# Pooled attention and a top-1 expert layer on one core: where the experts' tiles start in SBUF, when the second slot's weights are split, and where the last slots' tests stand

## The chip, the cores and the metric

The kernel runs on one core of a Trainium2 chip. The core has five engines that run side by side: TensorE (PE in the profile; its weight loads are PEld), VectorE (DVE), ScalarE (ACT), GpSimd (POOL) and SyncE (SP, which here only starts transfers). The on-chip memory SBUF has 128 partitions; PE writes its results to PSUM, in banks of 512 float32 per partition. The metric is the device time of one execution in microseconds (us), the median of several runs.

## The reference

Two layers follow each other. Attention over 8 batches, 8 heads, 576 rows of 64 numbers: keys and values are averaged over groups of 8 rows, and each query attends to the 72 averages. Its output, 4608 tokens of 512 numbers, goes through a layer of 8 experts, of which each token takes one:

```python
logits = x @ w_gate + modality_bias[modality_id]
e_idx = np.argmax(logits, axis=1)
...
gate_w = probs[np.arange(N), e_idx]
for e in range(E):
    mask = e_idx == e
    ...
    h = np.maximum(x[mask] @ w1[e], 0.0)
    out[mask] = gate_w[mask, None] * (h @ w2[e])
```

w1 of an expert is 512 x 1024, w2 is 1024 x 512. With the inputs given, only three experts get tokens: expert 6 gets 2289, expert 7 gets 1186, expert 1 gets 1133. The first token belongs to expert 6.

## The kernel before

**Attention and routing** fill the first part of the program (lines 190 to 1028). Attention writes its rows to a buffer in device memory (xs), and routing numbers each token's place among the tokens of its expert.

**Slots.** The experts' part works in slots of 256 tokens of one expert. Slots of one expert follow each other; the first expert is that of token 0, the others come in rotation. The first two slots (EARLY_SLOTS) are filled from the tokens routed first, so that they can start before all of attention is done. Up to 27 slots are provided for; how many are used is known only at run time. With these inputs the last used one (number 17) takes 256 tokens and up to 128 more, and is called the wide slot below (function wide).

**Precision by parts.** A float32 product is built from three products of rounded parts. A tile is split into a high part (rounded copy) and a low part (the difference to the original): for weights hl[f][:, 0] and hl[f][:, 1], for tokens the two parts of xhl, for activations hh and hlo.

**One slot** runs over eight blocks f of 128 hidden units. For each f:
- first_wide: four matmuls (line 186, high weights times both parts of the tokens, 512 columns) and four (line 189, low weights times the high part, 256 columns) into a PSUM bank hp. Then ACT copies one half (L191), DVE adds the other (L192), ACT applies the ReLU and rounds (L193, tile hh), DVE writes the rest (L195, tile hlo).
- second, one f behind: for each of two 128-token tiles, three matmuls (line 1239) with hh, hh and hlo as the stationary tile and the high, low and high part of w2's block as the moving one, 512 columns, accumulated over f into a bank op.
So PE runs hidden(f), second(f-1), hidden(f+1), and so on; the chain L191, L192, L193, L195 for f has the time of second(f-1) and hidden(f+1) to finish. The wide slot uses line 176 in the place of 186 and 189, with 384 columns; its activations for f from 3 on are kept in tiles hx, those before in hh and hlo.

**Around it.** A slot's tokens are gathered by POOL (L142), scaled by POOL (L153), transposed by PE (L166) and split by ACT (L168) and DVE (L169) into xhl while the slot before runs, at f=5 or 6. Even slots use xhl0, odd ones xhl1. A slot's outputs are scaled (L1210 on DVE, L1212 on ACT) and scattered to the output by POOL (L1216).

**Weights.** The raw weights of the next slot's expert are loaded by SP into raw, and split in place for the next slot as soon as a block has been used: renew(f) puts split_hi (L136, ACT) right away, and split_lo (L139, DVE) together with the next load into a list, lag, one entry of which is taken at each following step. From slot 2 on, the split stands under a condition: flags[s+1], loaded by slot_flag into registers of ACT and DVE (L1193), says whether slot s+1 has another expert than slot s. In slot 1 the splits are always done:

```python
        def changed(fn):
            if s < EARLY_SLOTS:
                fn()
                return
            with tc.If(flags[s + 1] > 0, preferred_fallthrough_block=False):
                fn()
```

**Small work with a fixed place.** Routing's last steps and the tables of token numbers are a list of operations by place, late[(slot, f)], issued by do_late right after hidden(f). At (2, 1) stands a DVE comparison over 1584 elements (L1100), and at (3, 5) 22 small DVE operations, halves + last_half, which say how the last slots are to be run. Their results are read at the end of the program only.

**Order.** [...]

**Places in SBUF.** A pool lays its tiles out one behind the other, each rounded up to 32 bytes. Per partition, the tiles that matter start at these bytes: xhl0 26272 (160 modulo 512); xhl1 149056 (64); hh0, hh1, hlo0, hlo1 from 165504 in steps of 1536 (128); hx from 184032 in steps of 1536 (224); hl, the split weights, from 83520 in steps of 8192 (64). xhl1, hh and hlo are wide enough for the wide slot, so an ordinary slot leaves a gap in each of their rows. The experts' tiles lie over those of attention, which are done with by then.

Of the kernel before, what the change touches and what calls it, by code (L numbers as in the profile page):

```python
# [31 lines left out]
def kernel(  # L32
# [16 lines left out]
    E, _, FF = w1.shape  # L49
# [17 lines left out]
    cp = ctx.enter_context(tc.tile_pool(name="cp", bufs=1))  # L67
# [19 lines left out]
        raw[f] = cp.tile([P, 2 * D], F32, tag=f"raw{f}", name=f"raw{f}")  # L87

    xg = [cp.tile([P, XW], F32, name=f"xg{i}") for i in range(4)]
    xhl = [cp.tile([P, ND, 2, SLOT], F32R, name="xhl0")]  # L90
    arow = cp.tile([P, NT, P], BF16, name="arow")
    oh = cp.tile([P, NT, E], BF16, name="oh")
    cum = cp.tile([P, len(GROUPS) + 1, E], BF16, name="cum")
    gate = cp.tile([P, NT], F32, name="gate")
    rh = cp.tile([P, NT], F32, name="rh")
    idw = cp.tile([P, 2, NT], BF16, name="idw")
    gidx = cp.tile([P, NCOL], I32, name="gidx")
# [5 lines left out]
    adjv = cp.tile([P, E], F32, name="adjv")  # L103
    e0oh = cp.tile([P, E], F32, name="e0oh")
    lmat = cp.tile([P, E, E], F32, name="lmat")
    tri = cp.tile([P, P], BF16, name="tri")
    ones = cp.tile([P, P], BF16, name="ones")
    sel0 = cp.tile([P, P], BF16, name="sel0")
    sc1 = cp.tile([P, NT, E], F32, name="sc1")
# [46 lines left out]
    def scale(s, xgs):  # L156
        for tt in range(2):
            scale_tile(xgs[(2 * s + tt) % 4])

    def x_transposes(s, xgs, tts=(0, 1)):  # L160
        ab = xhl[s % len(xhl)]
        for tt in tts:
            x = xgs[(2 * s + tt) % 4] if tt < 2 else xgs[4]
            pt = ps_tr.tile([P, ND, P], F32, tag="tr", name=f"xt_{s}_{tt}")
            for d in range(ND):
                nc.tensor.transpose(pt[:, d, :], x[:, d * P:(d + 1) * P], ident)  # L166
            sl = slice(tt * P, (tt + 1) * P)
            nc.scalar.copy(ab[:, :, 0, sl], pt)  # L168
            nc.vector.tensor_sub(ab[:, :, 1, sl], pt, ab[:, :, 0, sl].bitcast(F32))  # L169
# [41 lines left out]
    with ExitStack() as actx:  # L211
# [737 lines left out]
        for n in range(N + 1):  # L949
            has, nxt, nxt2 = n < N, n + 1 < N, n + 2 < N  # L950
# [80 lines left out]


    mp = ctx.enter_context(tc.tile_pool(name="mp", bufs=1))
    xhl.append(mp.tile([P, ND, 2, SLOT + P], F32R, name="xhl1"))
    xg.append(mp.tile([P, XW], F32, name="xe"))
    xe = xg[4]
    ps_hp = ctx.enter_context(tc.tile_pool(name="ps_hp", bufs=1, space=PSUM))
    ps_op = ctx.enter_context(tc.tile_pool(name="ps_op", bufs=1, space=PSUM))
    op = [[ps_op.tile([P, 512], F32, name=f"op{i}_{z}") for z in range(2)] for i in range(2)]
    hp = [ps_hp.tile([P, 512], F32, name=f"hp{i}") for i in range(2)]  # L1040
    hts = [mp.tile([P, SLOT], F32, name=f"ht{i}") for i in range(2)]
    hhs = [mp.tile([P, SLOT + P], F32R, name=f"hh{i}") for i in range(2)]
    hlos = [mp.tile([P, SLOT + P], F32R, name=f"hlo{i}") for i in range(2)]


    cf = mp.tile([P, E], F32, name="cf")
# [106 lines left out]
    for i, r in enumerate(EXTRA):  # L1153
# [19 lines left out]
        (0, 5): lr[21:] + columns,  # L1173
        (1, 0): first_cols[:3] + changes,
        (1, 2): first_cols[3:],
        (3, 5): halves + last_half,
    }
    t = table(c4 + 6, NCOL, 4)
    for i, at_ in enumerate(((2, 1), (2, 3), (2, 5), (2, 7), (3, 0), (3, 1), (3, 2))):
        late[at_] = t[i:i + 1]  # L1180
# [15 lines left out]

    def part(s):

        ab = xhl[s % 2]
        o = op[s % 2]  # L1200
        third = op[(s + 1) % 2][0]
        nxt, nxt2 = s + 1 < NSLOT, s + 2 < NSLOT
        early = s + 1 < EARLY_SLOTS
# [37 lines left out]

        def changed(fn):

            if s < EARLY_SLOTS:
                fn()
                return
            with tc.If(flags[s + 1] > 0, preferred_fallthrough_block=False):  # L1247
                fn()

# [12 lines left out]

        def first_next():
            if nxt:
                first_wide(0, xhl[(s + 1) % 2], hp[0], hts[0], hhs[0][:, 0:SLOT], hlos[0][:, 0:SLOT])

        def slot0(tail):
            for f in range(NF):
# [11 lines left out]
        def run(fs, tail):  # L1280
            later = []
            for f in fs:
                def pop():
                    if len(lag) > 1 or (f == 1 and lag):
                        lag.pop(0)()
                if f:
                    hidden(f, between=pop)
                if f == 0:

                    if 0 < s < NSTAT - 1:  # L1290
                        tail(later=later)
                    else:
                        tail()
                    if nxt and EARLY_SLOTS <= s < NSTAT - 1:
                        gather(s + 1, gidx, 2 * (s + 1), xg)
                        if s == NSTAT - 2:
                            gather_tile(xe, gidx, 2 * NSTAT)
                if f == 0:
                    pop()
                do_late(s, f)  # L1300
                if f == 0 and nxt and not early and s >= EARLY_SLOTS:
                    slot_flag(s + 1)
                if f == 0 and nxt2:
                    slot_regs(s + 2)
                if s == 1 and f == 2:
                    gather(s + 1, gidx, 2 * (s + 1), xg)

                if s >= NSTAT - 1 and f == CUT and nxt:
                    gather(s + 1, gidx, 2 * (s + 1), xg)
                if f:  # L1310
                    second(f - 1)
                    renew(f - 1)
                if f == (3 if EARLY_SLOTS <= s < NSTAT - 1 else 4) and nxt and not early:
                    scale(s + 1, xg)
                    if s == NSTAT - 2:
                        scale_tile(xe)
                    while later:
                        later.pop(0)()
                if s == NSTAT - 2 and f == 4:
                    nc.gpsimd.drain()  # L1320
                if f == (5 if EARLY_SLOTS <= s < NSTAT - 1 else 6) and nxt:
                    x_transposes(s + 1, xg)
                if s == NSTAT - 2 and f == 6:
                    x_transposes(s + 1, xg, (2,))
                if f == NF - 1 and s != NSTAT - 2:
                    close()
# [37 lines left out]
        def wide(extra, close_last, tail):  # L1364

            W = SLOT + extra
            nc.vector.tensor_copy(sl, sidx[:, 2 * (s + 1):2 * (s + 1) + 1])
            at = {f: hx[f - CUT] if f >= CUT else None for f in range(NF)}
            close_last(lambda: hidden(0, at[0], W))
            tail()  # L1370
            lag.pop(0)()
            for f in range(1, NF):
                hidden(f, at[f], W)
                if lag:
                    lag.pop(0)()
                second(f - 1, (0,) if f > CUT else (0, 1, 2), at[f - 1], W)
            second(NF - 1, (0,), at[NF - 1], W)
            evac((0,))
            for tt in (1, 2):
                for f in range(CUT, NF):  # L1380
                    second(f, (tt,), at[f], W)
                if tt == 1:
                    evac((1,))
            gt = xe[0:extra, D:D + 1]
            nc.vector.tensor_scalar_mul(obl[0:extra], third[0:extra], gt)  # L1385

        return slot0 if s == 0 else run, end, evac, end_half, close, wide

    CUT = 3
    hx = [[mp.tile([P, SLOT + P], F32R, name=f"hx{i}_{z}") for z in range(2)] for i in range(NF - CUT)]  # L1390

    obl = mp.tile([P, D], F32, name="obl")
    nc.gpsimd.memset(obl, 0.0)
# [85 lines left out]
```

## Time and profile before

| | us |
|---|---|
| median of 3 runs (lowest, highest) | 619.83 (618.6, 620.39) |
| profiled execution, its own time | 619.8 |
| its span, first to last instruction | 618.1 |
| PE busy | 594.4 (96%) |
| PE weight loads busy | 511.7 (83%) |
| DVE busy | 350.0 (57%) |
| ACT busy | 280.5 (45%) |
| POOL busy | 227.9 (37%) |

In the profile's rows a matmul's length is longer than the distance to the next one, since matmuls overlap; where rates are meant, distances between starts are used. In a row of a group stand line, engine, operation, tiles written and read, shape and count, then the engine's busy time, the mean length of one in ns, and the idle time ahead of them with what ended it. In a row of the timeline stand start, length, engine and line, and in brackets the idle time before. In a row of windows stand the stretch, its length, each engine's busy time with its number of instructions, the granted PE clock, the share of the transfer engines, and GB/s. Attention takes the first 185 us or so; the slots follow from there to the end.

### The profile page before, as it was taken

The numbers are of one execution on the slowest core, as the hardware profiler recorded it, in microseconds if no ns is written. First come the engines' busy times: TensorE is split into PE (matmuls) and PEld (weight loads), VectorE is DVE, ScalarE is ACT, GpSimd is POOL, SyncE is SP. The second block draws the span as 40 slices with busy tenths as digits, with TensorE's granted clock in tenths as the row PEclk, the third lists the DMA queues.
The fourth block names the chain that finished last, engine by engine and source line by source line (L and its number), as shares of the span: only waits on it lengthen the run. The fifth ranks groups of instructions, "written<-read, shape, count | busy, mean of one in ns | idle before, by whom it ended". The sixth has DMA issues, their size and how long they took to land.

```text
span 618.1 us, 12163 instructions
## 1 busy us (share of the span) xinstructions
PE 594.4 (96%) x3663; PEld 511.7 (83%) x3663; DVE 350.0 (57%) x823; ACT 280.5 (45%) x661; POOL 227.9 (37%) x325
## 2 busy tenths in 40 slices
PE   5899999999999999999999999999999999999996
PEld 4789889888898877878888888888888888888894
DVE  6757898789958786454344345744344476434311
ACT  2667676788541553333333336433333563333210
POOL 7689969663000351403313304304304214215101
PEclk9999999999999999999999999999999999999999
DMA  9999979884202820102102155102105611102001
GB/s 248 298 307 308 361 196 367 276 266 131 65 36 79 266 69 36 54 17 71 37 34 71 50 191 172 37 32 70 37 35 159 206 48 58 35 37 86 36 2 54
DMA packets 61104, 76.33 MB, mean 123 GB/s; under 512 B 15391, under 2 KB 39967, under 8 KB 61024
## 3 DMA queue, kind: packets, MB, share of 16 engines
q1 hardware_dynamic: 55104, 55.98, 29.1%
q0 software_dynamic: 5920, 19.44, 9.6%
q8 instruction: 31, 0.51, 0.3%
q14 instruction: 49, 0.40, 0.2%
HBM read 114.94 MB, written 19.45 MB: 217 GB/s over the span
## 4 chain that ended last, share of the span: by engine, by line
PE 55%; POOLq 0%; issue 0%; DVE 0%; DVEq 0%
PE op L1239 27%; PE hp L186 16%; PE hp L189 8%; PE hp L176 3%; PE xt L166 2%; POOLq L1474 0%; DVE obl L1385 0%; DVEq L1385 0%; POOLq L1446 0%
## 5 line engine op out<-in xcount | busy, mean ns | idle before, releaser
L1239 PE MATMUL op<-hl,hh 128*128 128x512 f32 x530 | 167.1, 396 | 1.4 <-ACTq L1247 1.4
L186 PE MATMUL hp<-xhl,hl 128*128 128x512 f32 x512 | 141.0, 397 | 0.0
L192 DVE TENSOR_TENSOR ht<-ht,hp 128x256 f32<-128x256 f32 x128 | 53.9, 421 | 125.2 <-ACT ht L191 124.9
L142 POOL DMA_INDIRECT xg<-xs,gidx x36 | 39.4, 1094 | 203.2 <-ACT ht L191 138.1
L191 ACT COPY ht<-hp 128x256 f32<-128x256 f32 x128 | 47.7, 373 | 143.1 <-PE hp L189 142.8
L186 PEld LDWEIGHTS hp<-xhl,hl 128*128 128x128 f32 x512 | 94.8, 188 | 21.1
L1239 PE MATMUL op<-hl,hlo 128*128 128x512 f32 x265 | 105.2, 397 | 1.6 <-DVE hlo L195 1.5
L1239 PEld LDWEIGHTS op<-hl,hh 128*128 128x128 f32 x530 | 91.0, 188 | 13.5 <-ACTq L1247 1.6
L195 DVE SCALAR_TENSOR_TENSOR hlo<-ht,hh 128x256 fp32r<-128x256 f32 x128 | 65.9, 514 | 52.5 <-ACTq L1247 46.2
L189 PEld LDWEIGHTS hp<-xhl,hl 128*128 128x128 f32 x512 | 78.4, 188 | 11.5
L193 ACT ACTIVATE hh<-ht 128x256 fp32r<-128x256 f32 x128 | 53.5, 418 | 72.1 <-DVE ht L192 72.1
L189 PE MATMUL hp<-xhl,hl 128*128 128x256 f32 x512 | 81.5, 281 | 0.0
L1216 POOL DMA_INDIRECT out_dram<-ob,sidx x36 | 39.9, 1107 | 77.0 <-DMA out_dram<-ob,sidx 51.3
L1239 PEld LDWEIGHTS op<-hl,hlo 128*128 128x128 f32 x265 | 49.8, 188 | 15.8 <-DVE hlo L195 4.1
L638 PE MATMUL av<-vw,pt 128*128 128x146 f32 (+1 forms) x320 | 49.7, 294 | 2.3 <-DVE xb L671 1.2
L153 POOL TENSOR_TENSOR xg<-xg 128x512 f32<-128x512 f32 x32 | 36.1, 1131 | 31.6 <-DMA xg<-xs,gidx 31.4
L638 PEld LDWEIGHTS av<-vw,pt 128*128 128x128 f32 (+1 forms) x320 | 39.7, 180 | 4.8 <-ACT pt L608 2.2
L139 DVE TENSOR_TENSOR hl<-raw,hl 128x1024 fp32r<-128x1024 f32 x32 | 39.6, 1246 | 0.0
L574 PE MATMUL sc<-kt,qt 128*128 128x144 f32 x256 | 37.3, 289 | 1.0 <-ACT qt L555 1.0
L574 PEld LDWEIGHTS sc<-kt,qt 128*128 128x128 f32 x256 | 33.1, 190 | 1.7 <-ACT qt L555 0.9
L581 DVE TENSOR_REDUCE mx<-sc 128x8 f32<-128x576 f32 (+1 forms) x40 | 27.7, 691 | 8.9 <-PE sc L574 6.8
L642 PE MATMUL av<-vw,pt 128*128 128x146 f32 (+1 forms) x160 | 30.7, 291 | 0.3
(257 smaller groups left out, 821.7 us busy)
## 6 DMA issues: line engine op xcount, KB each, us to landing
raw<-in_moe_w_dram SPq DMA_DIRECT2D x288, 256.0 KB
xs<-xb SPq DMA_DIRECT2D x16, 528.0 KB
k<-in_k_dram SPq DMA_DIRECT2D x7, 1024.0 KB
v<-in_v_dram SPq DMA_DIRECT2D x7, 1024.0 KB
q<-in_q_dram SPq DMA_DIRECT2D x7, 1024.0 KB
v<-in_v_dram SPq DMA_DIRECT2D x16, 128.0 KB
xs<-xb SPq DMA_DIRECT2D x8, 132.0 KB
k<-in_k_dram SPq DMA_DIRECT2D x4, 256.0 KB
```

The source lines that it names most:

```text
L139: eng.tensor_sub(hl[f][:, 1, :], raw[f], hl[f][:, 0, :].bitcast(F32))
L142: nc.gpsimd.indirect_dma_start(out=x, out_offset=None, in_=xs[0:rows, :], in_offset=IndirectOffsetOnAxis(idx[:, col:col + 1].bitcast(U32), 0),
L186: nc.tensor.matmul(ph, hl[f][:, 0, d * P:(d + 1) * P], ab[:, d, :, 0:SLOT], start=(d == 0), stop=False)
L189: nc.tensor.matmul(ph[:, 0:SLOT], hl[f][:, 1, d * P:(d + 1) * P], ab[:, d, 0, 0:SLOT], start=False, stop=(d == ND - 1))
L191: nc.scalar.copy(t, ph[:, SLOT:2 * SLOT])
L192: nc.vector.tensor_add(t, t, ph[:, 0:SLOT])
L193: nc.scalar.activation(hh, t, AF.Relu)
L195: nc.vector.scalar_tensor_tensor(hlo, t, 0.0, hh.bitcast(F32), op0=ALU.max, op1=ALU.subtract)
L574: nc.tensor.matmul(dst, qt[:, i, :], kt[b % NB][:, :, h * SPL:(h + 1) * SPL], start=True, stop=True)
L638: nc.tensor.matmul(av[hs, u, 2 * VC * gg:2 * VC * (gg + 1)], pt[:, c, hs], vw[y][:, c].rearrange("p a x -> p (a x)"), start=(gg == 0), sto ...
L1216: nc.gpsimd.indirect_dma_start(out=out[:, :], out_offset=IndirectOffsetOnAxis(idx.bitcast(U32), 0), in_=ob, in_offset=None, bounds_check=N ...
L1239: nc.tensor.matmul(ot, l[:, ts_], hl[f][:, w, D:2 * D], start=(f == 0 and n == 0), stop=(f == NF - 1 and n == 2))
```

## The change

It has three parts.

1. **Starts of tiles.** The tiles gate (144 bytes, taking 160) and tri (256 bytes) move ahead of xhl0, which then starts at 26688, 64 modulo 512. xhl1, hh and hlo lose the extra 128 columns of the wide slot and so the gaps; the wide slot gets its own token tile xw, its activations for f before 3 go to two pairs of tiles hy, and xe, the extra rows' buffer, moves behind them. By these sizes xhl1, ht, hh, hlo, xw, hx and hy all start at 64 modulo 512. As hy has two pairs, the wide slot's order changes in one point: the three matmuls of f=2 for the third token tile move from behind hidden(3) to the end.
2. **The second slot's splits.** Slot 1's splits go under the same condition as those of later slots; the flag for slot 2 is loaded at f=1 of slot 1.
3. **The tests.** halves + last_half are issued three at a time at (3, 4), (3, 6), (3, 7) and (4, 0) to (4, 4).

```diff
     xg = [cp.tile([P, XW], F32, name=f"xg{i}") for i in range(4)]
+    gate = cp.tile([P, NT], F32, name="gate")
+    tri = cp.tile([P, P], BF16, name="tri")
     xhl = [cp.tile([P, ND, 2, SLOT], F32R, name="xhl0")]
...
-    gate = cp.tile([P, NT], F32, name="gate")
...
-    tri = cp.tile([P, P], BF16, name="tri")
...
-        ab = xhl[s % len(xhl)]
+        ab = xhl[s % len(xhl)] if s != NSTAT - 1 else xw
...
-    xhl.append(mp.tile([P, ND, 2, SLOT + P], F32R, name="xhl1"))
-    xg.append(mp.tile([P, XW], F32, name="xe"))
-    xe = xg[4]
+    xhl.append(mp.tile([P, ND, 2, SLOT], F32R, name="xhl1"))
...
-    hhs = [mp.tile([P, SLOT + P], F32R, name=f"hh{i}") for i in range(2)]
-    hlos = [mp.tile([P, SLOT + P], F32R, name=f"hlo{i}") for i in range(2)]
+    hhs = [mp.tile([P, SLOT], F32R, name=f"hh{i}") for i in range(2)]
+    hlos = [mp.tile([P, SLOT], F32R, name=f"hlo{i}") for i in range(2)]
+    CUT = 3
+    xw = mp.tile([P, ND, 2, SLOT + P], F32R, name="xw")
+    hx = [[mp.tile([P, SLOT + P], F32R, name=f"hx{i}_{z}") for z in range(2)] for i in range(NF - CUT)]
+    hy = [[mp.tile([P, SLOT + P], F32R, name=f"hy{i}_{z}") for z in range(2)] for i in range(2)]
+    xg.append(mp.tile([P, XW], F32, name="xe"))
+    xe = xg[4]
...
-        (3, 5): halves + last_half,
     }
+    tests = halves + last_half
+    for i, at_ in enumerate(((3, 4), (3, 6), (3, 7), (4, 0), (4, 1), (4, 2), (4, 3), (4, 4))):
+        late[at_] = tests[3 * i:3 * i + 3]
...
         def changed(fn):
 
-            if s < EARLY_SLOTS:
-                fn()
-                return
             with tc.If(flags[s + 1] > 0, preferred_fallthrough_block=False):
                 fn()
...
-                if f == 0 and nxt and not early and s >= EARLY_SLOTS:
+                if f == (0 if s >= EARLY_SLOTS else 1) and nxt and not early:
                     slot_flag(s + 1)
...
-            at = {f: hx[f - CUT] if f >= CUT else None for f in range(NF)}
+            at = {f: hx[f - CUT] if f >= CUT else hy[f % 2] for f in range(NF)}
...
-                second(f - 1, (0,) if f > CUT else (0, 1, 2), at[f - 1], W)
+                second(f - 1, (0,) if f > CUT else (0, 1) if f == CUT else (0, 1, 2), at[f - 1], W)
...
-                for f in range(CUT, NF):
+                for f in range(CUT + 1 - tt, NF):
                     second(f, (tt,), at[f], W)
```

More of the change, by code (lines that the diff above doesn't have):

```diff
@@ L158, in scale @@
             scale_tile(xgs[(2 * s + tt) % 4])
+    xw = None
     def x_transposes(s, xgs, tts=(0, 1)):
-        ab = xhl[s % len(xhl)]
+        ab = xhl[s % len(xhl)] if s != NSTAT - 1 else xw
         for tt in tts:
@@ L1175 @@
         (1, 2): first_cols[3:],
-        (3, 5): halves + last_half,
     }
+    tests = halves + last_half
+    for i, at_ in enumerate(((3, 4), (3, 6), (3, 7), (4, 0), (4, 1), (4, 2), (4, 3), (4, 4))):
+        late[at_] = tests[3 * i:3 * i + 3]
+    assert len(tests) <= 24
     t = table(c4 + 6, NCOL, 4)
@@ L1197, in part @@
     def part(s):
-        ab = xhl[s % 2]
+        ab = xhl[s % 2] if s != NSTAT - 1 else xw
         o = op[s % 2]
@@ L1264, in first_next @@
             if nxt:
-                first_wide(0, xhl[(s + 1) % 2], hp[0], hts[0], hhs[0][:, 0:SLOT], hlos[0][:, 0:SLOT])
+                first_wide(0, xhl[(s + 1) % 2] if s + 1 != NSTAT - 1 else xw, hp[0], hts[0], hhs[0][:, 0:SLOT], hlos[0][:, 0:SLOT])
         def slot0(tail):
@@ L1387, in part @@
         return slot0 if s == 0 else run, end, evac, end_half, close, wide
-    CUT = 3
-    hx = [[mp.tile([P, SLOT + P], F32R, name=f"hx{i}_{z}") for z in range(2)] for i in range(NF - CUT)]
     obl = mp.tile([P, D], F32, name="obl")
```

## The prediction

> **What bounds the kernel now.** I read the page first, then the tensor engine's timeline, slot by slot, because the page leaves little doubt about the engine:
>
> ```profile
> span 618.1 us, 12163 instructions
> PE 594.4 (96%) x3663; PEld 511.7 (83%) x3663; DVE 350.0 (57%) x823; ACT 280.5 (45%) x661; POOL 227.9 (37%) x325
> ...
> PE op L1239 27%; PE hp L186 16%; PE hp L189 8%; PE hp L176 3%; PE xt L166 2%; POOLq L1474 0%; DVE obl L1385 0%; DVEq L1385 0%; POOLq L1446 0%
> ...
> L186 PEld LDWEIGHTS hp<-xhl,hl 128*128 128x128 f32 x512 | 94.8, 188 | 21.1
> ...
> L1239 PEld LDWEIGHTS op<-hl,hh 128*128 128x128 f32 x530 | 91.0, 188 | 13.5 <-ACTq L1247 1.6
> ```
>
> PE is busy 96% and the chain that ended last is PE matmuls. So time can only be won by shortening PE's own steps, or by closing the few places where PE stands still. The second kind is seen against a normal step of an odd slot (here in slot 9, PE rows of the timeline; first column start, second the group's length):
>
> ```profile
> 441.36 1.09 PE L186 MATMUL hp<-xhl,hl 128*128 128x512 f32 x4
> 442.28 0.64 PE L189 MATMUL hp<-xhl,hl 128*128 128x256 f32 x4
> 442.75 0.62 PE L1239 MATMUL op<-hl,hh 128*128 128x512 f32 x2
> 443.22 0.40 PE L1239 MATMUL op<-hl,hlo 128*128 128x512 f32 x1
> 443.45 0.63 PE L1239 MATMUL op<-hl,hh 128*128 128x512 f32 x2
> ```
>
> From start to start: four L189 take 0.47, two L1239 take 0.47, one takes 0.23. A larger distance is a stall. The lengths themselves overlap and are not used.
>
> **Part 1, the tests of the last slots are spread.** In slot 3 all 22 small DVE instructions sit at f=5, ahead of the activations' transposes (L169) and the next chain L191, L192, L193, L195. First and last of the 22 on DVE, what follows there, and PE:
>
> ```profile
> 264.84 0.16 DVE L1066 TENSOR_SCALAR cg<-cf 128x8 f32<-128x8 f32 x1
> ...
> 268.51 0.14 DVE L1162 CAST meta<-lhs 1x1 int32<-1x1 f32 x1
> ...
> 270.01 0.41 DVE L192 TENSOR_TENSOR ht<-ht,hp 128x256 f32<-128x256 f32 x1
> 270.90 0.43 DVE L195 SCALAR_TENSOR_TENSOR hlo<-ht,hh 128x256 fp32r<-128x256 f32 x1 [0.48 <-ACTq L1247]
> ```
> ```profile
> 268.91 0.63 PE L189 MATMUL hp<-xhl,hl 128*128 128x256 f32 x4
> 270.92 0.73 PE L1239 MATMUL op<-hl,hh 128*128 128x512 f32 x2 [1.38 <-ACTq L1247]
> 271.49 0.39 PE L1239 MATMUL op<-hl,hlo 128*128 128x512 f32 x1
> ```
>
> The tests hold DVE for 268.65-264.84 = 3.81 us. PE goes from L189 to L1239 in 2.01 instead of 0.47, and the pair that follows takes 0.57 instead of 0.47: 1.54+0.10 = **1.64 us lost**. After the change three tests, 3 x 3.81/22 = 0.52 us, stand at each of eight steps. They hide in DVE's idle time ahead of the next L192; the tightest of these places, slot 4 f=2, has
>
> ```profile
> 282.93 0.42 DVE L192 TENSOR_TENSOR ht<-ht,hp 128x256 f32<-128x256 f32 x1 [0.70 <-ACT ht L191]
> ```
>
> 0.70 us, more than 0.52. Without that cover, PE would lose at most 0.52 us at a step. Nothing reads the tests' results before the end of the program, so nobody waits for the later ones. I take the whole 1.64; bounds 1.1 (one step uncovered) and 1.64.
>
> **Part 2, slot 1's splits under a condition.** The split of a weight tile is L136 on ACT and L139 on DVE. Its bursts:
>
> ```profile
> L136 ACT CAST hl<-raw x24: 1031/1050/1052, 203.9 to 508.9; 128x1024 fp32r<-128x1024 f32 x24
> ...
> busy tenths in 40 slices 0000000000000320000000003200000130000000
> ```
>
> Eight in slot 1, always done, and two bursts later where the expert changes. The reference with its inputs sends 2289 tokens to expert 6 (the first token's), 1186 to 7, 1133 to 1. Expert 6 fills slots 0 to 8, so slot 2 has slot 1's expert, the flag is 0, and the eight splits rewrite weights that are there already. The change drops 8 x 1.05 us on ACT and 8 L139 on DVE. Off PE that is worth only what PE waited for:
>
> ```profile
> 213.59 1.22 DVE L139 TENSOR_TENSOR hl<-raw,hl 128x1024 fp32r<-128x1024 f32 x1
> 214.72 1.27 DVE L195 SCALAR_TENSOR_TENSOR hlo<-ht,hh 128x256 fp32r<-128x256 f32 x1
> ...
> 227.66 1.80 DVE L1100 TENSOR_TENSOR bsel<-iota_f,col 128x1584 bf16<-128x1584 f32 x1
> 229.38 0.42 DVE L192 TENSOR_TENSOR ht<-ht,hp 128x256 f32<-128x256 f32 x1
> 229.71 1.74 DVE L139 TENSOR_TENSOR hl<-raw,hl 128x1024 fp32r<-128x1024 f32 x1
> 231.38 1.26 DVE L195 SCALAR_TENSOR_TENSOR hlo<-ht,hh 128x256 fp32r<-128x256 f32 x1
> ```
> ```profile
> 215.38 0.63 PE L1239 MATMUL op<-hl,hh 128*128 128x512 f32 x2
> 216.04 0.50 PE L1239 MATMUL op<-hl,hlo 128*128 128x512 f32 x1
> 216.38 0.63 PE L1239 MATMUL op<-hl,hh 128*128 128x512 f32 x2
> ```
> ```profile
> 230.59 0.63 PE L1239 MATMUL op<-hl,hh 128*128 128x512 f32 x2
> 232.69 0.50 PE L1239 MATMUL op<-hl,hlo 128*128 128x512 f32 x1 [1.46 <-DVE hlo L195]
> 233.02 0.63 PE L1239 MATMUL op<-hl,hh 128*128 128x512 f32 x2
> ```
>
> First place (slot 1): 0.66-0.47 and 0.34-0.23, that is 0.19+0.11. Second (slot 2, f=2's correction hlo): 2.10-0.47 and 0.33-0.23, 1.63+0.10. Together **2.03 us**. What is late next is read from ACT's two L191 of slot 2, f=1 and f=2:
>
> ```profile
> 225.29 0.36 ACT L191 COPY ht<-hp 128x256 f32<-128x256 f32 x1
> ...
> 228.04 0.37 ACT L191 COPY ht<-hp 128x256 f32<-128x256 f32 x1 [1.31 <-PE hp L189]
> ```
>
> From L192 to L195 it is 0.89 (rows of part 1), L195 takes 0.43. Without its three L139, DVE ends L195 of f=1 at 225.65+0.89+0.43 = 227.0, L1100 at 228.8, and runs L192 of f=2 from there, since L191 is done at 228.4; L195 starts at 229.7. PE needs it at 231.06 (230.59+0.47). Even at the 1.26 us of the quoted row it ends at 231.0, so the wait is gone or within 0.1. GpSimd, which scales tokens at that time,
>
> ```profile
> 229.33 1.04 POOL L153 TENSOR_TENSOR xg<-xg 128x512 f32<-128x512 f32 x1 [1.04 <-DMA xg<-xs,gidx]
> ```
>
> is done at 230.37; were L195 held until then, it would end at 230.8, still in time.
>
> The added wait: at f=1 of slot 1, ACT and DVE load the flag,
>
> ```profile
> L1193 ACTq TENSOR_LOAD <-meta x15: 273/276/473, 223.8 to 556.2; - x15
> ```
>
> 0.3 to 0.5 us, behind L193 and L195 of that step. Behind it stands the next L191 or L192, which waits for PE about as long; and slots 2 to 7 carry the same load and the same branches with no stall of PE. Cost 0; up to 0.2 if the load is late. Bounds of part 2: 0.3 (only the first place goes) to 2.03.
>
> **Part 3, the starts of the tiles.** In the allocation of the kernel before, every weight tile hl and the odd slots' xhl1 start at 64 modulo 512 bytes, the even slots' xhl0 at 160, hh and hlo at 128, hx at 224. After, all are at 64. The windows of slots 4 and 5, cut at the first L186 of each slot, show what goes with it:
>
> ```profile
> 272.42:295.77 23.35, 23.35 (x122) 19.68 (x120) 9.57 (x19) 7.99 (x20) 6.29 (x6) 1.00 0.14 47
> 295.77:318.99 23.22, 23.22 (x122) 19.64 (x121) 9.15 (x19) 8.11 (x20) 6.28 (x6) 1.00 0.14 48
> ```
>
> The same work at the same clock takes 23.35 in the even slot, 23.22 in the odd one: 0.13 us. If that is xhl0's start, eight even slots (2 to 16) win 8 x 0.13 = **1.0 us**. For hh, hlo and hx the nearest rows are matmuls alone with stationaries at 128 (first) and at 224 (second):
>
> ```profile
> 590.65 2.10 PE op L1239 x9
> ...
> 604.78 7.16 PE L1239 MATMUL op<-hl,hx 128*128 128x512 f32 x30
> ```
>
> 2.10/9 = 233 ns; and (7.16-0.40)/29 = 233 ns, the last one's 0.40 taken off. Two starts, one rate: I cost the stationaries' move at 0. Bounds: L186, whose stationary and (in odd slots) moving tile both start at 64, takes (442.28-441.36)/4 = 230 ns; if L1239 came to that, 3.3 ns x 840 of them in slots 1 to 17 = 2.8 us would be won, of which I allow half, 1.4, since part of the difference is where a group begins. Below, no gain in xhl0 and the odd slots as slow as the even ones: 1.0 lost. So part 3 lies between -2.4 and +1.0, and I take -1.0, the row of the very tile that moves.
>
> [...]
>
> **The rest costs nothing.** In the wide slot three L1239 move from before the first output's scatter to the end: the count on PE is the same, and the output rows in between leave 0.7 us earlier on idle engines. The new places of obl and ob lie over attention's row buffers, whose last stores must have landed before they are written. Were the first ob late, PE would meet it only when it writes the same output bank again, a slot (23 us) later.
>
> **Sum.** 1.64+2.03+1.0 = 4.7. The profiled execution has span 618.1 and its own time 619.8, so 1.7 us lie around the span. 619.8-4.7 = **615.1**. It stands 0.03 under the median of the runs, 619.83.
>
> **Rivals.**
> 1. Starts do not matter; the slot's parity does, through the output banks. For: those alternate with the slot too. Against: the nine L1239 in a row write three banks at one rate. 619.8-3.7 = 616.1. [...]
> 2. The common start helps L1239 as well: 619.8-3.67-2.4 = 613.7. For: L186's 230 ns. Against: the equal 233 at 128 and 224.
> 3. Slot 2's stall remains because L1100 alone is long enough, or another wait takes its place: 1.7 less gain, 616.8. Against: the 1.2 us of room worked out above.
> 4. The gap in xhl1's rows, not its start, made odd slots fast; closing it makes all slots slow: 619.8-3.67+1.0 = 617.1.
> 5. Slower than before: stationary and moving tile at one residue get in each other's way, the weight load outgrows its matmul and PE waits for loads at every L1239. Now 188 ns lie under 233. From a load of 233+3.67/840 = 238 ns the gain is gone; at 250 ns it costs 17 x 840 = 14 us, 630. Against: L186's loads start at 64 and take the same 188.
>
> **How the numbers follow.** Forecast 0.48, with its own range 614.4 to 615.8; rival 1 0.16, rival 2 0.16, rival 3 0.09, rival 4 0.08, rival 5 0.03. The range from 613.0 to 617.6 holds all but rival 5 and the tails. A measurement here cannot tell 0.3% (1.9 us) from no change, as the runs of before spread from 618.6 to 620.39. Faster by more, under 618.0: 0.92, all but rival 5 and a quarter of 3 and 4; within: 0.05; slower: 0.03.
>
> **What would show it.** Right: L136 16 times, none before slot 8; no PE distance over 0.5 us between L189 and L1239 in slot 3, nor between hh and hlo in slot 2; tests on DVE in threes; even slots at 23.2. Wrong: a stall at another line of slots 1 to 4; odd slots at 23.35; L1239 in a row off 233 ns; weight loads over 188 ns. A time above 617.6 or below 613.0 would mean that the tiles' starts act on PE in a way these rows do not have.

## The result and the profile after

The changed kernel takes 611.19 us (median of 4 runs, 609.76 to 611.62) beside 620.11 us (4 runs, 618.6 to 620.83) of the kernel before: a ratio of 0.9855 with a 95% interval of 0.983 to 0.9881. That is 8.9 us less where 4.7 were forecast, and the time lies under the forecast's own range (614.4 to 615.8) and under the 613.0 to 617.6 that held most of the rivals. In the profiled executions the span falls from 618.1 to 609.8 us, by 8.3.

The page after (span; busy time of PE). In the changed kernel's numbering L186, L189, L192, L195 and L1239 are L188, L191, L194, L197 and L1248, and L1100 is L1106:

```profile
span 609.8 us, 12218 instructions
...
PE 590.1 (97%) x3663; PEld 512.3 (84%) x3663; DVE 339.1 (56%) x815; ACT 273.1 (45%) x653; POOL 225.2 (37%) x325
```

PE issues as many matmuls as before, 3663, and is still the bound. So the gain is standing still that went, or matmuls that follow each other faster. Both are there.

**The three stalls are gone.** The PE rows of the timeline at the places the prediction quoted: slot 1, slot 2 and slot 3.

```profile
215.29 0.63 PE L1248 MATMUL op<-hl,hh 128*128 128x512 f32 x2
215.76 0.39 PE L1248 MATMUL op<-hl,hlo 128*128 128x512 f32 x1
...
230.02 0.63 PE L1248 MATMUL op<-hl,hh 128*128 128x512 f32 x2
230.49 0.39 PE L1248 MATMUL op<-hl,hlo 128*128 128x512 f32 x1
...
266.34 0.64 PE L191 MATMUL hp<-xhl,hl 128*128 128x256 f32 x4
266.81 0.63 PE L1248 MATMUL op<-hl,hh 128*128 128x512 f32 x2
267.28 0.39 PE L1248 MATMUL op<-hl,hlo 128*128 128x512 f32 x1
```

Each distance is 0.47 us, the normal one; they were 0.66, 2.10 and 2.01. On DVE in slot 2, where the long comparison and a low split had stood ahead of hlo:

```profile
226.41 1.80 DVE L1106 TENSOR_TENSOR bsel<-iota_f,col 128x1584 bf16<-128x1584 f32 x1
228.13 0.41 DVE L194 TENSOR_TENSOR ht<-ht,hp 128x256 f32<-128x256 f32 x1
229.03 0.53 DVE L197 SCALAR_TENSOR_TENSOR hlo<-ht,hh 128x256 fp32r<-128x256 f32 x1 [0.48 <-ACTq L1253]
```

L197 ends at 229.56, and the matmul that needs it starts at 230.49. The splits themselves (the rows of L136):

```profile
L136 ACT CAST hl<-raw x16: 1047/1050/1052, 366.0 to 502.0; 128x1024 fp32r<-128x1024 f32 x16
...
busy tenths in 40 slices 0000000000000000000000003200000130000000
```

Sixteen, none before slot 8.

**Ordinary steps are shorter, in even and odd slots alike.** The windows of slots 4 and 5, cut at the slot's first matmul as in the prediction:

```profile
268.20:291.22 23.02, 23.02 (x122) 19.65 (x121) 11.85 (x35) 8.11 (x20) 6.43 (x6) 1.00 0.15 48
291.22:314.24 23.02, 23.02 (x122) 19.65 (x121) 9.02 (x19) 8.11 (x20) 6.32 (x6) 1.00 0.15 48
```

The forecast had the even slot come down from 23.35 to the odd one's 23.22. Both are at 23.02. One step of an odd slot, PE's timeline:

```profile
291.22 1.07 PE L188 MATMUL hp<-xhl,hl 128*128 128x512 f32 x4
292.12 0.64 PE L191 MATMUL hp<-xhl,hl 128*128 128x256 f32 x4
292.60 0.63 PE L1248 MATMUL op<-hl,hh 128*128 128x512 f32 x2
...
293.98 1.07 PE L188 MATMUL hp<-xhl,hl 128*128 128x512 f32 x4
```

The odd step that the prediction quoted (it is one of slot 11, where the prediction says slot 9) ends with this row of before:

```profile
444.15 1.09 PE L186 MATMUL hp<-xhl,hl 128*128 128x512 f32 x4
```

The six L1248 take 293.98-292.60 = 1.38 us, 230 ns each, where that step had 444.15-442.75 = 1.40; the four L188 take 0.90 instead of 0.92. A step is 2.76 to 2.77 us, against 2.79 in odd slots before and 2.81 in even ones (in slot 10 the L186 start at 412.42 and 415.23).

A step is a better unit than a line in it. By the starts of single matmuls in slot 5, an odd step is shorter by 27 ns, of which 19 lie in the four L188, 1 in the four L191 and 6 in the six L1248. The pair of tiles of L188 started equal in odd slots before the change too, so what a line gains depends on its neighbours.

**Attention is untouched.** The first output matmul of slot 0 starts at 184.89 us in both profiles. DVE's last instruction on the output starts here before and here after:

```profile
612.41 0.75 DVE L1385 TENSOR_SCALAR obl<-op,xe 128x512 f32<-128x512 f32 x1 [6.68 <-PE op L1239]
```
```profile
604.18 0.75 DVE L1391 TENSOR_SCALAR obl<-op,xe 128x512 f32<-128x512 f32 x1 [6.83 <-PE op L1248]
```

So 8.23 of the 8.3 us lie in the experts' part. About 0.4 of them lie behind PE: that DVE instruction starts 0.87 us after the start of the last matmul before and 0.49 after. From the first output matmul to the start of the last one it is 7.86 us less.

### The profile page after: what moved, and what is told of

It reads as the page before. It is cut to its first block, busy times and chain, and to the rows that moved or that the text cites. A ratio compares the mean times of both kernels' runs of the same rounds, so it can differ in the third digit from the quotient of the medians.

```text
span 609.8 us, 12218 instructions
## 1 busy us (share of the span) xinstructions
PE 590.1 (97%) x3663; PEld 512.3 (84%) x3663; DVE 339.1 (56%) x815; ACT 273.1 (45%) x653; POOL 225.2 (37%) x325
## 4 chain that ended last, share of the span: by engine, by line
PE 78%; DVE 7%; POOL 5%; DMA 5%; ACT 2%; issue 2%; SPq 0%; POOLq 0%; DVEq 0%; ACTq 0%
PE op L1248 32%; PE hp L188 18%; PE hp L191 10%; DMA k<-in_k_dram 5%; PE av L640 3%; PE hp L178 3%; PE xt L168 2%; PE av L644 2%; PE sc L576 2%; PE ph L178 1%; PE pp L605 1%; POOL k L325 1%; PE pq L551 1%; DVE hl L139 1%; POOL v L325 1%
## 5 line engine op out<-in xcount | busy, mean ns | idle before, releaser
L1248 PE MATMUL op<-hl,hh 128*128 128x512 f32 x512 | 161.0, 396 | 0.0
L188 PE MATMUL hp<-xhl,hl 128*128 128x512 f32 x512 | 138.8, 393 | 0.0
L194 DVE TENSOR_TENSOR ht<-ht,hp 128x256 f32<-128x256 f32 x128 | 53.9, 421 | 124.3 <-ACT ht L193 121.2
L142 POOL DMA_INDIRECT xg<-xs,gidx x36 | 38.1, 1057 | 197.8 <-ACT ht L193 120.6
L188 PEld LDWEIGHTS hp<-xhl,hl 128*128 128x128 f32 x512 | 94.8, 188 | 19.2
L1248 PE MATMUL op<-hl,hlo 128*128 128x512 f32 x256 | 100.1, 391 | 0.2
L1248 PEld LDWEIGHTS op<-hl,hh 128*128 128x128 f32 x512 | 87.9, 190 | 11.3 <-ACT hh L195 0.3
L197 DVE SCALAR_TENSOR_TENSOR hlo<-ht,hh 128x256 fp32r<-128x256 f32 x128 | 63.3, 495 | 55.8 <-ACTq L1253 49.0
L191 PEld LDWEIGHTS hp<-xhl,hl 128*128 128x128 f32 x512 | 78.2, 189 | 10.3
L195 ACT ACTIVATE hh<-ht 128x256 fp32r<-128x256 f32 x128 | 53.6, 419 | 67.5 <-DVE ht L194 67.1
L191 PE MATMUL hp<-xhl,hl 128*128 128x256 f32 x512 | 81.2, 281 | 0.0
L1248 PEld LDWEIGHTS op<-hl,hlo 128*128 128x128 f32 x256 | 48.1, 188 | 12.6 <-DVE hlo L197 1.6
L153 POOL TENSOR_TENSOR xg<-xg 128x512 f32<-128x512 f32 x32 | 35.5, 1115 | 32.4 <-DMA xg<-xs,gidx 32.2
L139 DVE TENSOR_TENSOR hl<-raw,hl 128x1024 fp32r<-128x1024 f32 x24 | 29.0, 1219 | 0.4 <-issue 0.4
```

What stands on the lines that cost most here:

```text
L142: nc.gpsimd.indirect_dma_start(out=x, out_offset=None, in_=xs[0:rows, :], in_offset=IndirectOffsetOnAxis(idx[:, col:col + 1].bitcast(U32), 0),
L188: nc.tensor.matmul(ph, hl[f][:, 0, d * P:(d + 1) * P], ab[:, d, :, 0:SLOT], start=(d == 0), stop=False)
L191: nc.tensor.matmul(ph[:, 0:SLOT], hl[f][:, 1, d * P:(d + 1) * P], ab[:, d, 0, 0:SLOT], start=False, stop=(d == ND - 1))
L194: nc.vector.tensor_add(t, t, ph[:, 0:SLOT])
L195: nc.scalar.activation(hh, t, AF.Relu)
L197: nc.vector.scalar_tensor_tensor(hlo, t, 0.0, hh.bitcast(F32), op0=ALU.max, op1=ALU.subtract)
```

## The experiments

In other executions attention took up to 2 us more or less (the first output matmul came between 183.9 and 186.7 us). The table therefore has the experts' part alone beside the span: from that matmul to the start of the last DVE instruction on the output, both read in the timeline.

| kernel | span | experts' part | slots 4 and 5 | ratio of the times to before, same job (95%) |
|---|---|---|---|---|
| before | 618.1 | 427.52 | 23.35, 23.22 | |
| changed | 609.8 | 419.29 | 23.02, 23.02 | 0.9855 (0.983 to 0.9881) |
| tests only | 616.3 | 426.21 | 23.35, 23.21 | 0.9964 (0.9944 to 0.9983) |
| condition only | 617.5 | 425.08 | 23.31, 23.20 | 0.9963 (0.9943 to 0.9983) |
| starts only | 613.1 | 423.29 | 23.02, 23.02 | 0.9934 (0.990 to 0.9968) |
| changed, activations 64 on | 611.9 | 422.37 | 23.22, 23.21 | 0.9918 (0.989 to 0.9946) |
| changed, activations 256 on | 611.3 | 419.01 | 23.02, 23.01 | one run |
| changed, gaps back | 609.4 | 418.97 | 23.01, 23.02 | one run |
| changed, xhl0 at 160 | 609.9 | 420.11 | 23.12, 23.02 | one run |
| changed, low weights 16 on | 609.6 | 419.70 | 23.00, 23.02 | 0.9884 (0.9862 to 0.9907) |

Kernels that should be alike (changed, 256 on, gaps back) differ by 0.3 us in the experts' part, and the three kernels below that put groups behind the changed kernel's end by up to 0.7 (418.94 to 419.67). The traces show from what. Where the next expert's weights are split, two to four steps of a run take 3.1 us, because the writing of hlo (L195, L197 after) takes 1.27 us there instead of 0.42, with GpSimd's scaling of tokens (L153) at work at the same time (in before, hlo at 398.02, 494.25 and 515.02, GpSimd's rows from 397.71, 494.13 and 514.44, 2.48, 1.10 and 2.75 us long), and PE waits for it. There are three such steps in before and in changed, four with the tests only and with the low weights 16 on, two with 256 on and gaps back, and three in the other rows. So 0.3 us of a difference can be one such step more or less. The other irregular piece is the 0.4 us behind the last matmul: tests only has it as before, and all other rows have lost it, the condition alone and the starts alone among them. By what, no run shows.

### One part at a time

The theory after the first comparison: the two stall terms are right, and the tiles' starts are worth 4.6 us instead of 1.0. The rival: the three parts need each other.

```diff
-        (3, 5): halves + last_half,
     }
+    tests = halves + last_half
+    for i, at_ in enumerate(((3, 4), (3, 6), (3, 7), (4, 0), (4, 1), (4, 2), (4, 3), (4, 4))):
+        late[at_] = tests[3 * i:3 * i + 3]
```

> The kernel before with the tests spread and nothing else. Reading of the two traces: the stall of 1.54+0.10 us in slot 3 goes and nothing else changes, so 1.6 us less (span 616.5). Rival: the tests' removal from f=5 moves a wait elsewhere in slots 3 and 4, then less than 1.1 us is won.

The ratio is 0.9964, 2.2 us less (by the 95% interval 1.1 to 3.5). PE in slot 3 of this kernel (its L1242 is L1239):

```profile
268.47 0.63 PE L189 MATMUL hp<-xhl,hl 128*128 128x256 f32 x4
268.94 0.63 PE L1242 MATMUL op<-hl,hh 128*128 128x512 f32 x2
269.41 0.39 PE L1242 MATMUL op<-hl,hlo 128*128 128x512 f32 x1
```

2.01 has become 0.47 and 0.57 has become 0.47: 1.64 us, as worked out. The experts' part is shorter by 1.31, and this run has one more of the 0.3 us waits at the splits. No stall came up in slots 3 and 4.

```diff
         def changed(fn):
-            if s < EARLY_SLOTS:
-                fn()
-                return
             with tc.If(flags[s + 1] > 0, preferred_fallthrough_block=False):
...
-                if f == 0 and nxt and not early and s >= EARLY_SLOTS:
+                if f == (0 if s >= EARLY_SLOTS else 1) and nxt and not early:
```

> The kernel before with slot 1's splits under the condition and nothing else. Reading of the two traces: the stalls of 0.30 us in slot 1 and 1.73 us in slot 2 go, 2.0 us less (span 616.1). Rival: the missing splits are worth more than the stalls, because ACT and DVE also free PE's later steps; then over 2.5 us.

The ratio is 0.9963, 2.3 us (1.1 to 3.5). PE in slot 2:

```profile
231.39 0.63 PE L1239 MATMUL op<-hl,hh 128*128 128x512 f32 x2
231.86 0.39 PE L1239 MATMUL op<-hl,hlo 128*128 128x512 f32 x1
232.09 0.63 PE L1239 MATMUL op<-hl,hh 128*128 128x512 f32 x2
```

The wait of 1.63+0.10 is gone. The experts' part is 2.44 us shorter, of which 0.37 lie behind the last matmul; the other 2.07 are the stalls' 2.03. The missing splits bring nothing beyond the stalls that can be told.

For the starts alone, both edits above were taken back out of the changed kernel:

> The changed kernel with the splits of slot 1 always done and the 22 tests at one place again, so that only the tiles' starts and sizes are changed. If the three parts add up, 8.3-1.64-2.03 = 4.6 us of span are left here (span 613.5), and a step of an ordinary slot takes 2.767 us. Rival: the starts alone are worth the 1.0 us of the forecast (span 617.1, steps of 2.793) and the rest needs all three parts together.

The ratio is 0.9934, 4.1 us (2.0 to 6.2), the experts' part 4.23 us shorter, both slots at 23.02. The rival falls: the starts alone do it. One thing does not add: with a faster PE and the splits still there, the stall in slot 2 grows,

```profile
229.63 0.63 PE L1245 MATMUL op<-hl,hh 128*128 128x512 f32 x2
231.99 0.50 PE L1245 MATMUL op<-hl,hlo 128*128 128x512 f32 x1 [1.73 <-DVE hlo L197]
```

to 2.36-0.47 = 1.89 from 1.63. DVE there:

```profile
226.83 1.80 DVE L1106 TENSOR_TENSOR bsel<-iota_f,col 128x1584 bf16<-128x1584 f32 x1
...
228.88 1.87 DVE L139 TENSOR_TENSOR hl<-raw,hl 128x1024 fp32r<-128x1024 f32 x1
230.67 1.26 DVE L197 SCALAR_TENSOR_TENSOR hlo<-ht,hh 128x256 fp32r<-128x256 f32 x1
```

About half of the 0.26 us is that PE arrives earlier, 3.27 us after the start of L1106 (229.63+0.47-226.83) where it was 3.40 after that of L1100; the other half is that the chain on DVE is longer, 5.10 instead of 4.98 us, with a split of 1.87 instead of 1.74. The three experts' parts together give 1.31+2.44+4.23 = 7.98 of 8.23. To the last matmul, and with the extra wait of the tests' run and the longer stall of this one set right, they give 1.6+2.07+4.1 = 7.8 of 7.86.

### What about the starts: one matmul by itself

Behind the end of the changed kernel, groups of 32 matmuls take one weight tile as stationary and another as moving tile, each with a chosen start; their results go to no output, so that the run's whole time says nothing.

```diff
+    def probe(g, st, mv, n, count):
+        wt = hl[0].rearrange("p w c -> p (w c)")[:, st // 4:st // 4 + P]
+        mt = hl[1].rearrange("p w c -> p (w c)")[:, mv // 4:mv // 4 + n]
+        for _ in range(count):
+            nc.tensor.matmul(hp[g % 2][:, 0:n], wt, mt, start=True, stop=True)
```

> The changed kernel with 48 groups of 32 matmuls behind its end, whose results go to no output: one weight tile as stationary, another as moving tile, with the stationary's start moved in steps of 64 or 32 bytes and the moving tile's start at 64, 0, 160 or 128 modulo 512. Theory S: with the moving tile at 64, a matmul of 512 columns takes 226.7 ns with the stationary at 64 and 233.3 ns at 128 and 224. Theory R: only the difference of the two starts counts, so that 226.7 ns is found wherever both are equal, also at 0, 128 and 160. Theory A: the stationary's absolute start counts whatever the moving tile's. Theory N (gaps, not starts): all groups take the same.

Windows of this run, one group of 32 each (stretch, its length, PE's busy time). Stationary and moving start, modulo 512, are 64/64, 128/64, 192/64, 256/64, 320/64, then 0/0, 64/160 and 128/128:

```profile
602.39:609.65 7.26, 7.26 (x34) 6.01 (x33) 0.75 (x1) 0.00 (x0) 0.97 (x1) 1.00 0.11 39
609.65:617.11 7.46, 7.46 (x33) 6.01 (x32) 0.00 (x0) 0.00 (x0) 0.00 (x0) 1.00 0.00 0
617.11:624.55 7.44, 7.44 (x33) 6.04 (x32) 0.00 (x0) 0.00 (x0) 0.00 (x0) 1.00 0.00 0
624.55:631.88 7.33, 7.33 (x34) 6.01 (x32) 0.00 (x0) 0.00 (x0) 0.00 (x0) 1.00 0.00 0
631.88:639.15 7.27, 7.27 (x33) 6.01 (x32) 0.00 (x0) 0.00 (x0) 0.00 (x0) 1.00 0.01 2
...
713.10:720.38 7.28, 7.28 (x34) 6.01 (x32) 0.00 (x0) 0.00 (x0) 0.00 (x0) 1.00 0.00 0
720.38:727.84 7.46, 7.46 (x34) 6.00 (x33) 0.00 (x0) 0.00 (x0) 0.00 (x0) 1.00 0.01 2
787.48:794.75 7.27, 7.27 (x34) 6.01 (x32) 0.00 (x0) 0.00 (x0) 0.00 (x0) 1.00 0.00 0
```

Divided by 32, and with the starts of single matmuls for the last 20 of each group: 226.7 ns where the two starts are equal (64/64, 0/0, 128/128) or 256 apart (320/64), 233.4 with the stationary 64 bytes on, 232.4 at 128, 228.8 at 192, and 233 to 234 at every odd multiple of 32. With the moving tile at 0, 64 or 128 the same difference gives the same time. Theory R holds, with modulo 256: for these 512-column matmuls the difference counts, neither start by itself. Theory S came true as the case of it with the moving tile at 64. Theories A and N fall.

This also says why the forecast's two rows agreed. In the kernel before, hh stood 64 bytes after the moving weights (128 against 64) and hx 160 after (224 against 64). Both are slow differences, 233.4 and 233.2 ns in this run. The two rows were two samples of the slow rate.

### The same in the kernel

```diff
+    mp.tile([P, 16], F32, name="shift")
     hhs = [mp.tile([P, SLOT], F32R, name=f"hh{i}") for i in range(2)]
     hlos = [mp.tile([P, SLOT], F32R, name=f"hlo{i}") for i in range(2)]
+    mp.tile([P, 112], F32, name="back")
     CUT = 3
     xw = mp.tile([P, ND, 2, SLOT + P], F32R, name="xw")
+    mp.tile([P, 16], F32, name="shift2")
     hx = [[mp.tile([P, SLOT + P], F32R, name=f"hx{i}_{z}") for z in range(2)] for i in range(NF - CUT)]
```

> The changed kernel with hh, hlo, hx and hy 64 bytes further on (128 modulo 512), all else at 64. Theory R (the difference of stationary and moving start modulo 256 sets a matmul's rate): L1248 goes back to 233 ns, an ordinary step from 2.767 to 2.793 us, and of the 4.6 us that the starts brought 128 x 0.026 = 3.3 us are lost again (span 613). Theory X (the start of xhl0 alone, as forecast): nothing is lost, span 609.8.

Slots 4 and 5 of this kernel:

```profile
267.61:290.83 23.22, 23.22 (x122) 19.64 (x120) 11.74 (x35) 8.09 (x20) 6.22 (x6) 1.00 0.15 47
290.83:314.04 23.21, 23.21 (x121) 19.62 (x120) 9.17 (x19) 8.09 (x20) 6.19 (x6) 1.00 0.15 47
```

Both are where the odd ones of before were: 0.2 us a slot is lost again, and 3.08 us of the experts' part, with as many of the 0.3 us waits as in the changed kernel. This kernel is also the forecast's own case, xhl0 moved and the activations not in step: even slots fall from 23.35 to 23.22, 8 x 0.13 = 1.0 us, and nothing more.

The same with 64 and 64 elements in the place of 16 and 112, so that the activations are 256 bytes on:

> The changed kernel with hh, hlo, hx and hy 256 bytes further on (320 modulo 512), all else at 64. Theory R: the difference is 0 modulo 256, so steps stay at 2.767 us and the span at 609.8. Theory F (64 modulo 512 is what counts): steps of 2.793 us, span 613.

```profile
269.98:293.00 23.02, 23.02 (x122) 19.65 (x121) 11.67 (x35) 8.09 (x20) 6.23 (x6) 1.00 0.15 48
```

23.02: no loss. The activations start at 320 modulo 512 here, so "64 modulo 512" is not what matters. The span of 611.3 comes from attention: the first output matmul starts at 186.66 in this execution, and the experts' part takes 419.01.

```diff
-    xhl.append(mp.tile([P, ND, 2, SLOT], F32R, name="xhl1"))
+    xhl.append(mp.tile([P, ND, 2, SLOT + P], F32R, name="xhl1"))
...
-    hhs = [mp.tile([P, SLOT], F32R, name=f"hh{i}") for i in range(2)]
-    hlos = [mp.tile([P, SLOT], F32R, name=f"hlo{i}") for i in range(2)]
+    hhs = [mp.tile([P, SLOT + P], F32R, name=f"hh{i}") for i in range(2)]
+    hlos = [mp.tile([P, SLOT + P], F32R, name=f"hlo{i}") for i in range(2)]
```

> The changed kernel with xhl1, hh and hlo as wide as before, so that their rows have gaps again, while all starts are still at 64 modulo 512. Theory R: steps of 2.767 us, span 609.8. Theory G (the gaps cost, not the starts): steps of 2.793 us and over, span 613.

Slots take 23.01 and 23.02 and the span is 609.4. These gaps, 512 bytes wide, cost nothing; rival 4 of the prediction falls.

Then gate and tri behind xhl0 again, so that xhl0 is at 160 and the rest as in the changed kernel:

> The changed kernel with gate and tri behind xhl0 again, so that xhl0 starts at 160 modulo 512 and all else at 64. Theory R: the matmuls of even slots with xhl0 as moving tile lose their equal start; by the whole steps run alone (2.780 against 2.767 us) even slots take 0.1 us more, odd ones stay, and the span grows by 8 x 0.1 = 0.8 us to 610.6. That is then what the forecast's 1.0 us was worth. Theory W (even slots were slow as a whole because of xhl0, 0.3 us each between 23.35 and 23.03): span grows by 2.6 us.

```profile
267.57:290.69 23.12, 23.12 (x121) 19.64 (x120) 11.66 (x35) 8.07 (x20) 6.21 (x6) 1.00 0.14 47
290.69:313.71 23.02, 23.02 (x121) 19.65 (x120) 9.27 (x19) 8.10 (x20) 6.18 (x6) 1.00 0.15 48
```

Even slots lose 0.10, odd ones none, and the experts' part grows by 0.82, with as many of the 0.3 us waits as the changed kernel. Theory W falls: xhl0's start is worth 0.8 to 1.0 us.

### Is there a better difference for the 256-column matmuls?

The first run of groups had 256-column matmuls at 120.0 ns at difference 0 and 117.8 at 64, so equal starts need not suit L191. A second run of groups, again behind the end and to no output, took those, and whole steps of 4 matmuls of 512, 4 of 256 and 6 of 512 columns:

```diff
+    def step(i, low, act, tok):
+        for d in range(4):
+            mm(hp[i % 2], 512 * d, 2048 * (d % 3) + tok, 512)
+        for d in range(4):
+            mm(hp[i % 2], 512 * d + low, 2048 * (d % 3) + tok, 256)
+        for tt in range(2):
+            for w in range(3):
+                mm(op[0][tt], 512 * tt + act, 2048 * (w % 2), 512)
```

> The changed kernel with groups of matmuls behind its end, whose results go to no output: 256 columns with the stationary 0 to 240 bytes after the moving tile in steps of 16; 512 columns at 16 to 240 in steps of 32; and whole steps of 4 matmuls of 512, 4 of 256 and 6 of 512 columns with chosen differences. Theory R: 512 columns at 233 ns at every difference that is not a multiple of 64; a step with all differences 0 takes 2.767 us, with L1248 at 64 2.793 us, with L1248 at 64 and the tokens 96 bytes further on 2.813 us. The 256-column matmuls had 120.0 ns at difference 0 and 117.8 at 64 in the run before: if low weights with a difference of their own make a step shorter than 2.767 us, a version with that layout beats the changed kernel by 136 times as much; if whole steps do not shorten, none does.

Windows of eight steps each: all starts equal; low weights 16 on; activations 64 on; activations 64 and tokens 96 on; tokens 96 on:

```profile
726.91:749.04 22.13, 22.13 (x114) 18.83 (x112) 0.00 (x0) 0.00 (x0) 0.00 (x0) 1.00 0.00 1
749.04:771.12 22.08, 22.08 (x114) 18.77 (x112) 0.00 (x0) 0.00 (x0) 0.00 (x0) 1.00 0.00 1
948.61:970.95 22.34, 22.34 (x114) 18.80 (x113) 0.00 (x0) 0.00 (x0) 0.00 (x0) 1.00 0.00 1
970.95:993.45 22.50, 22.50 (x113) 18.86 (x112) 0.00 (x0) 0.00 (x0) 0.00 (x0) 1.00 0.00 1
993.45:1015.70 22.25, 22.25 (x114) 18.82 (x112) 0.00 (x0) 0.00 (x0) 0.00 (x0) 1.00 0.00 1
```

An eighth of each is 2.766, 2.760, 2.793, 2.813 and 2.781 us. Third and fourth are the odd and the even step of the kernel before to the nanosecond, with no other engine at work: starts alone make them. Theory R expected 233 ns at every difference that is no multiple of 64; it held at 16, 48, 112 and 144 (233.3 ns), not quite at 80 (232.0), 176 (230.0) and 208 (232.1), and not at 240, where 226.7 was reached as at 0. Ten values for the low weights gave one gain, 6.7 ns a step at 16 bytes. A version with that layout, in the six blocks for which there was room:

```diff
+    PADDED = (2, 3, 4, 5, 6, 7)
+    LOW = 4
+    def low(f):
+        if f not in PADDED:
+            return hl[f][:, 2 * D:4 * D].rearrange("p (z c) -> p z c", z=2)
+        pitch = D + 64 - LOW
+        return hl[f][:, 4 * D + 64 - 2 * pitch:4 * D + 64].rearrange("p (z c) -> p z c", z=2)[:, :, pitch - D:pitch]
...
-                hl[f] = big.tile([P, 2, 2 * D], F32R, tag=f"s{f}", name=f"hl{f}")
+                hl[f] = big.tile([P, 4 * D + 64 * (f in PADDED)], F32R, tag=f"s{f}", name=f"hl{f}")
```

> The changed kernel with the low parts of w1 (stationary of the 256-column matmuls) 16 bytes on against the tokens' start modulo 256 in six of eight blocks f, all other starts equal modulo 256. The same whole step run alone took 2.760 instead of 2.767 us: if that carries over, 6 x 17 x 6.7 ns = 0.7 us less than the changed kernel, span 609.1, with steps of 2.760. If the order of neighbours in the kernel undoes it (the steps alone alternated the same matmuls, without transposes and waits between), the span stays at 609.8.

The steps do come down, f=2 to f=4 to 2.760 us. But the step with the restart after the transposes grows from 2.855 to 2.878 (both in slot 5), so that a slot takes 23.00 and 23.02, as before. 611.44 us beside the changed kernel's 611.19, in two jobs: no gain that can be told.

### Which reads get in each other's way?

```diff
+    def group(sts, mvs, cols=P):
+        for i in range(32):
+            st, mv = sts[i % len(sts)] // 4, mvs[i % len(mvs)] // 4
+            nc.tensor.matmul(hp[0][0:cols, :], wt[:, st:st + cols], mt[:, mv:mv + 512], start=True, stop=True)
```

> The changed kernel with groups of 32 matmuls of 512 columns behind its end, results to no output; stationary and moving starts alternate between two values, and in a second part the stationary has only 32, 64 or 96 of its 128 columns. [...]

Windows of 32 matmuls, starts counted from those of the two weight tiles: both starts 0; stationary 64; both alternating 0, 64; stationary 0, 64 against moving 64, 0; then 32 columns of stationary at 0, and at 32:

```profile
602.88:610.13 7.25, 7.25 (x34) 6.01 (x32) 0.75 (x1) 0.00 (x0) 0.97 (x1) 1.00 0.11 39
610.13:617.59 7.46, 7.46 (x33) 6.02 (x32) 0.00 (x0) 0.00 (x0) 0.00 (x0) 1.00 0.00 0
617.59:625.01 7.42, 7.42 (x33) 6.01 (x32) 0.00 (x0) 0.00 (x0) 0.00 (x0) 1.00 0.00 0
625.01:632.47 7.46, 7.46 (x33) 6.01 (x32) 0.00 (x0) 0.00 (x0) 0.00 (x0) 1.00 0.00 0
661.95:669.35 7.40, 7.40 (x34) 3.48 (x33) 0.00 (x0) 0.00 (x0) 0.00 (x0) 1.00 0.01 2
676.76:684.39 7.63, 7.63 (x34) 3.48 (x32) 0.00 (x0) 0.00 (x0) 0.00 (x0) 1.00 0.00 0
```

Weight loads overlap matmuls here: in the first window the load is busy 6.01 us of 7.25, and PE all of it. If the load of the next matmul slowed the one under way by its start, stationaries that equal the moving tile under way but not their own would be fast, and a shorter load would help. Neither shows: such starts stay at 233.3 ns, and with a quarter of the columns, which keeps the load busy 3.48 instead of 6.01 us, the equal pair is slower, 231.7 ns instead of 226.7, and the one 32 bytes on takes 240. Nor does a matmul's own pair of starts alone set its time: alternating equal pairs take 231.7, not 226.7, so what the neighbours do counts too.

The other groups of this run fit neither reading. Starts that alternate by 32 or 128 against the moving tile's take 230.0, faster than 233.3 and 232.4 for a single pair that far apart, and slower than an equal one. With a narrower stationary equal starts lose most of their advantage over a start 64 bytes on: the two take 231.7 and 231.7 with 32 columns, 230.3 and 232.7 with 64, 230.0 and 228.4 with 96. By what mechanism the difference of starts acts is left open.

## Why the prediction was wrong, and where it was right

**Part 1 was right.** The tests' stall was put at 1.64 us and measured at 1.64 in its place; three tests fit under DVE's idle time at every new place (slot 4, with five of the eight places, takes 23.02 us, as slot 5 does).

**Part 2 was right.** 2.03 us at the two named places, both gone, and L195 of slot 2 ends well before PE needs it. The flag's load (0.27 to 0.47 us on ACT, 0.30 to 0.55 on DVE) and the added branches cost nothing that shows: the step of slot 1 in which the first load stands, from 201.81 us on, takes PE 3.79 us in both profiles.

**Part 3 failed**, in the step "Two starts, one rate: I cost the stationaries' move at 0". The term for xhl0, 1.0 us, was right (0.13 us for each even slot with the activations out of step, 0.10 with them in step). The term for hh, hlo, hx and hy was put at 0, with half of 2.8 us as its bound. The runs show 3.1 us in its place: so much the experts' part loses when these tiles alone stand 64 bytes further on, 0.20 us in an ordinary slot and 0.24 in the wide one. Of the 3.5 us between the 615.1 of the forecast and the 611.56 of the profiled execution, this is nearly all. The two rows quoted for the 0 are these in the changed kernel (nine L1248 in a row, and the last 15):

```profile
574.64 2.08 PE op L1248 x9
...
600.51 3.56 PE L1248 MATMUL op<-hl,hx 128*128 128x512 f32 x15
```

That is 2.08 where it was 2.10, and (3.56-0.39)/14 = 226 ns where it was 233. The inference from two places was of the wrong kind: equal rates at 128 and 224 show that these two do not differ, not that no start does. The question that the rows could have answered is what the pair of starts does. L186 in odd slots, both tiles at 64, was the one row with equal starts, and it was the fastest (230 ns). It was noted, as rival 2, and then halved on the ground that part of it is where a group begins. The runs do not bear the halving out: next to slow neighbours even the equal pair had not reached its 226.7 ns. Rival 2 with the whole difference gives 619.8-3.67-1.0-2.8 = 612.3, the nearest to 611.56. In the size that is partly luck, since rival 2 puts the gain into L1239, and in an odd step most of it came in the four matmuls of L186 (L188 after).

**The rivals.** Rival 1, starts without effect, falls with the groups: a 512-column matmul takes 226.7 or 233.4 ns by its starts alone. Rival 3 falls with part 2; the room that it calls 1.2 us is 0.93 by the prediction's own times (231.06-229.7-0.43), and 0.93 in the trace (230.49-229.56). Rival 4 falls with the kernel that has its gaps back. Rival 5 (whose 238 ns are 237 by its own sum) fails: equal starts are the fast case (226.7 ns), not a collision, and the mean length of a weight load stayed between 188 and 190 ns.

**The rest** was rightly put at nothing: the three moved matmuls (they start at 599.84, what follows them at 600.51) and the new places of obl and ob show no wait.

The sum from the measured terms: 1.64+2.03+1.0+3.1 = 7.8, as against 7.86 to the last matmul. The other 0.4 of the experts' 8.23 lies behind that matmul, and its cause stays open.

## What to carry to other kernels

Where matmuls of rounded float32 follow each other without a wait, as here, look at where stationary and moving tile start, modulo 256 bytes, and try a layout in which both are equal. Here, with a full 128-column stationary and 512 columns, that is 3% of a matmul by itself (226.7 against 233.4 ns) and 1% of a whole step (2.766 against 2.793 us), for no instruction at all; the groups show no such gain with 256 columns (120.0 against 117.8 ns with the stationary 64 bytes on), nor with a stationary of 32 (231.7 against 231.7), 64 (230.3 against 232.7) or 96 columns (230.0 against 228.4). Two slow samples that agree are no evidence that a parameter is without effect: before a term is put at 0, ask which value of the parameter none of the rows has. The stall in slot 2 was longer where PE arrived earlier (by 0.13 of the 0.26 us): a faster engine can make the stalls it still has longer.

## What the runs showed that was not expected

- In groups of 32 a 512-column matmul of rounded float32 took 226.7 ns when its two operands started equal modulo 256 bytes, and also with the stationary 240 bytes on; at the other multiples of 32 it took 228.8 to 234, and 240 at the worst with a 32-column stationary. The absolute starts tried made no difference (226.7 at 64/64, 0/0 and 128/128).
- Its neighbours counted. In slots with equal starts for L186 alone these took 230 to 232 ns, not 226.7; a group that came after another took up to seven matmuls to settle.
- For 256 columns equal starts were not the best: 120.0 ns, against 117.8 at 64 in one run and 113.4 in another (why the two differ is open). In whole steps run alone 64 brought nothing and 16 bytes 6.7 ns a step; in the kernel that was lost again in the step after the transposes.
- The lengths of whole steps, alone on PE, reproduce those of the kernel to the nanosecond (2.766, 2.793, 2.813 us), so such groups behind a kernel's end are a cheap way to try a layout.
